# Loading the last output weights of a decode kernel in 32 transfers of 8 partitions instead of 2 transfers of 128

## The chip, the cores and the metric

The kernel runs on one core of a Trainium2 chip. The metric is the device time of one execution in microseconds (us), median over several runs. The time before is 1278.78 us (three runs, 1278.07 to 1279.25).

## The reference

One decode step. Attention of one token over a cache of 65536 positions (8 KV heads, 2 query heads to each, head size 256), and beside it a gated feed-forward layer on the same normalised token; both results are added to the token.

```python
xn = layernorm(x)                                  # x: [1, 1, 448]
q = xn @ wq                                        # 16 heads of 256
p = softmax(q @ k_cache^T / 16)                    # k_cache, v_cache: [8, 65536, 256], bf16
o = p @ v_cache
out = x + o.reshape(1, 1, 4096) @ wo + ffn(xn)     # wo: [4096, 448]
```

K and V are 537 MB together, so the kernel is a stream of transfers from HBM. Of `wo`, the rows of the first 7 KV heads are loaded earlier; this study is about those of the last head, 448 KB, called `wo_end`.

## The kernel before

The parts that matter are at the end of the stream. V of the last head comes in pieces that get smaller, so that little work is left when the last one lands. `wo_end` comes behind them on the same queue (that of SP, the sync engine). The buffer `kt_all` that takes it is free long before.

```python
def item(key, parts, need=()):                     # queues transfers on SP
        for n in need:
            W("sp", *n)
        for ap, src, sem in parts:
            semtot[sem] = semtot.get(sem, 0) + 16
            items[key] = (sem, semtot[sem])
            prog["sp"].append(("d", here[0], ("DMA", key, len(prog["sp"])), (ap, src), sem))
# ...
def wo_src(h):
    return A_wo[h * rep * Dh:(h + 1) * rep * Dh, :].rearrange("(i p f) n -> p i f n", i=rep, f=NH)

def wo_view(t):
    return t.rearrange("p (i f n) -> p i f n", i=rep, f=NH)
# ... the queue's end; LAST = [64, 32, 16, 8, 4, 4], rep = 2, P = 128:
    slot_item("v", NT + 1, 1, None, [("FREE", NU - 1)])
    slot_item("v", NT + 2, 0, None, [("VFREE", NT)])
    slot_item("v", NT + 3, 2, [("last%d" % k if k < len(LAST) - 1 else "slot2", J) for k, J in enumerate(LAST)], [("ATTN",), ("FFN2",)])
    for i in range(rep):
        item(("wo_end", i), [(wo_view(wo_end)[:, i, :, :], wo_src(Hkv - 1)[:, i, :, :], "we%d" % i)],
             [("H", 0), ("H", 1)] if i == 0 else ())
# ... and how an entry of the queue is issued:
                eng.dma_start(fn[0], fn[1]).then_inc(sems[sem], 16)
```

The final product on PE (the TensorE) waits for the first half (semaphore `we0`), multiplies, waits for the second (`we1`) and multiplies again:

```python
        values(NT + 2)
        values(NT + 3)
        dve_ob(T)
        pe_oT(T)
        W("pe", "OTSB", T)
        for i in range(rep):
            W_item("pe", ("wo_end", i))

            def f(it, i=i):
                wo = wo_view(wo_end)
                for hf in range(NH):
                    for g in range(NF):
                        ins = mm(fin(g), lhsT=oT_sb[:, hf, i:i + 1], rhs=wo[:, i, hf, g * DQ:(g + 1) * DQ], start=False,
                                 stop=(i == rep - 1 and hf == NH - 1), tile_position=(0, 32 * g), skip_group_check=True)
                return ins

            O("pe", ("FIN", i), f)
        W("dve", "FIN", rep - 1)
```

Each `wo_end` transfer takes 128 rows of 1792 B, one to each partition. The profile of this kernel shows 256 packets of 1792 B for the two of them and, on each of `we0` and `we1`, 16 increments that came from DMA (1270.82 to 1272.80 and 1271.42 to 1273.36 us). The page counts 16 DMA engines, so this is read as one increment from each engine, after 8 rows. PE waits for 16.

## Time and profile before

| What | Value | Where it is read |
|---|---|---|
| time, median | 1278.78 us | timed runs |
| span of the profiled execution | 1276.0 us | page |
| last V transfer landed | 1272.23 us | semaphore records of the trace |
| `wo_end` landed, first and second half | 1272.80, 1273.36 us | semaphore records |
| from the last V to the last `wo_end` ("the tail") | 1.13 us | difference |

The page of the kernel before. The row DMA is the busy share of the 16 DMA engines in tenths, in 40 slices of the span; the last line is the chain of waits, by engine:

```profile
span 1276.0 us, 23620 instructions
...
DMA  9999999999999999999999999999999999999998
GB/s 405 430 428 440 437 431 436 431 429 440 433 429 438 427 440 433 431 438 427 436 436 431 438 429 431 438 431 431 438 427 438 436 431 438 427 436 438 409 434 360
DMA packets 13588, 549.20 MB, mean 430 GB/s; under 512 B 1414, under 2 KB 3464, under 8 KB 4104
...
DMA 76%; PE 19%; SPq 2%; ACT 1%; issue 1%; DVE 1%; ACTq 0%; DVEq 0%
```

The DMA engines are busy throughout, and the chain of work that ended last is three quarters DMA. So a change at the queue's end matters only through the last few microseconds. These are, in order of time, in the chain of waits of the kernel before (start, length, what; all in us):

```profile
by line: DMA ring<-in_A_v_cache_dram 82.2%; SPq L883 4.4%; PE ps_t L412 2.8%; PE ps_s L412 2.0%; PE ps_m L412 1.1%; issue 0.9%; DVE kt_all L835 0.8%; DVE oT_sb L654 0.4%; SPq L877 0.0%
...
1233.60 38.63 DMA ring<-in_A_v_cache_dram
...
1272.28 0.49 PE ps_m L412 x12
...
1273.02 0.94 PE ps_s L412 x8
...
1273.98 0.38 DVE kt_all L835
```

The last V, 0.5 us of PE, 0.2 us of DVE, then the final product with `wo_end` (`ps_s`). The timeline of the same stretch has the waits in brackets: the engine's idle time before the group, and what ended it.

```profile
1272.28 0.38 PE L412 MATMUL ps_m<-p_sb,ring 128*128 128x2 bf16 x8 [0.25 <-DMA ring<-in_A_v_cache_dram]
...
1272.80 0.16 DVE L654 TENSOR_TENSOR oT_sb<-ps_m,rs 128x4 bf16<-128x4 f32 x1 [0.48 <-PE ps_m L412]
...
1273.02 0.92 PE L412 MATMUL ps_s<-kt_all,oT_sb 128*1 128x224 bf16 x8 [0.25 <-DVE oT_sb L654]
1273.40 0.09 PEld L412 LDWEIGHTS ps_s<-kt_all,oT_sb 128*1 128x1 bf16 x4 [0.30 <-DMA kt_all<-in_A_wo_dram]
1273.98 0.38 DVE L835 CAST kt_all<-ps_s 33x224 bf16<-33x224 f32 x1 [1.02 <-PE ps_s L412]
```

The first half of the product starts as soon as its other operand `oT_sb` is there. The second half's weights waited 0.3 us for `wo_end`. In the list of waits, in us in total, times and longest:

```profile
PEld ps_s L412 <- DMA kt_all<-in_A_wo_dram: 0.3, 1, 0.3
```

And the two transfers by their tile (lengths of issue on SP in ns, minimum, median and maximum; then the time from issue to landing):

```profile
L883 SPq DMA_DIRECT2D kt_all<-in_A_wo_dram x2: 368/400/433, 1234.1 to 1234.5; - x2
...
DMA to landing us min/median/max: 38.7/38.7/38.8
```

So they are issued 38.7 us before they land: they queue behind V. The tail of 1.13 us is their own time on the engines, 16 packets each (75 ns a packet on average, 1.2 us). It is almost hidden behind the 0.7 us of work between V and the final product.

The 16 engines are not in step. From the semaphore records, the times at which each engine reported its share of the last V, and of the second `wo_end` transfer:

```
last V     1270.24 1270.37 1270.49 1270.94 1271.10 1271.52 1271.57 1271.75 1271.80 1271.82 1271.83 1271.87 1271.96 1272.01 1272.22 1272.23
wo_end, 2  1271.42 1271.56 1271.67 1272.08 1272.23 1272.60 1272.66 1272.84 1272.91 1272.93 1272.94 1272.95 1273.07 1273.12 1273.32 1273.36
```

Paired in order of time (the records don't name the engine), each ends 1.1 to 1.2 us after its own V. What counts is the slowest one.

### The profile page before, as it was taken

What the parts mean: (1) busy time and instruction counts of PE and PEld (TensorE: products, weight loads), DVE (VectorE), ACT (ScalarE), POOL (GpSimd) and SP (SyncE); (2) the same over time, 40 slices, a digit from 0 to 9 for tenths busy, and PEclk for the clock granted to TensorE, in tenths of its full rate; (3) what the DMA queues carried; (4) which work ended last, traced back from release to release, by engine and by line L of the source; (5) the groups of instructions that cost most, each with busy time, mean ns of one, the idle gap of its engine ahead of it and who ended that gap; (6) DMA issues with size and microseconds to landing.
All of it is one profiled execution on the core that took longest, in us unless ns stands there. A gap on an engine that the chain in (4) does not pass through costs nothing.

```text
span 1276.0 us, 23620 instructions
## 1 busy us (share of the span) xinstructions
PE 976.1 (76%) x9791; PEld 638.2 (50%) x9791; DVE 570.2 (45%) x1079; ACT 436.6 (34%) x655; POOL 8.0 (1%) x38
## 2 busy tenths in 40 slices
PE   4998888778777679767778776787777688777674
PEld 3676655455544456444555454455454455454321
DVE  4665554355444455343454344454344554444310
ACT  1554533244333334323333342343333334332300
POOL 2000000000000000000000000000000000000000
PEclk9998999799888898887898888898888998888885
DMA  9999999999999999999999999999999999999998
GB/s 405 430 428 440 437 431 436 431 429 440 433 429 438 427 440 433 431 438 427 436 436 431 438 429 431 438 431 431 438 427 438 436 431 438 427 436 438 409 434 360
DMA packets 13588, 549.20 MB, mean 430 GB/s; under 512 B 1414, under 2 KB 3464, under 8 KB 4104
## 3 DMA queue, kind: packets, MB, share of 16 engines
q1 hardware_dynamic: 13570, 549.03, 99.7%
q8 instruction: 8, 0.13, 0.0%
q14 instruction: 4, 0.03, 0.0%
q10 hardware_dynamic: 6, 0.00, 0.0%
HBM read 549.03 MB, written 0.00 MB: 430 GB/s over the span
## 4 chain that ended last, share of the span: by engine, by line
DMA 76%; PE 19%; SPq 2%; ACT 1%; issue 1%; DVE 1%; ACTq 0%; DVEq 0%
DMA ring<-in_A_v_cache_dram 70%; PE ps_o L412 13%; DMA ring<-in_A_k_cache_dram 5%; PE ps_t L412 3%; SPq L883 2%; PE ps_m L412 2%; PE ps_q L412 2%; ACT kt_all L482 1%; DMA ring<-in_A_wo_dram 1%; DVE kt_all L480 0%; ACT S_sb L563 0%; PE ps_s L412 0%; DVE kt_all L699 0%; DVE m1p L533 0%; DVE kt_all L835 0%
## 5 line engine op out<-in xcount | busy, mean ns | idle before, releaser
L412 PE MATMUL ps_t<-ident_f,ring 128*128 128x128 f32 x4096 | 590.0, 286 | 71.9 <-DMA ring<-in_A_k_cache_dram 48.3
L480 DVE COPY kt_all<-ps_t 128x1024 bf16<-128x1024 bf16 x768 | 486.9, 684 | 285.8 <-PE ps_q L412 281.2
L412 PEld LDWEIGHTS ps_t<-ident_f,ring 128*128 128x128 f32 x4096 | 453.9, 144 | 227.6 <-issue 139.8
L482 ACT ACTIVATE kt_all<-ps_t 128x1024 bf16<-128x1024 bf16 x256 | 262.2, 1024 | 507.0 <-PE ps_q L412 506.9
L412 PE MATMUL ps_o<-ring,p_sb 128*4 128x512 bf16 x2044 | 186.9, 531 | 195.6 <-DMA ring<-in_A_v_cache_dram 191.3
L412 PEld LDWEIGHTS ps_o<-ring,p_sb 128*4 128x4 bf16 x2044 | 55.2, 105 | 289.5 <-issue 265.7
L412 PE MATMUL ps_q<-kt_all,q_cur 128*2 128x512 bf16 x2056 | 164.7, 397 | 0.6 <-DVE kt_all L480 0.6
L504 ACT ACTIVATE s<-ps_q 98x512 bf16<-98x512 f32 x257 | 151.8, 591 | 1.3 <-PE ps_q L412 1.3
L588 DVE RECIPROCAL rs<-ps_m 128x4 f32<-128x4 f32 x29 | 5.3, 183 | 271.8 <-PE ps_m L412 271.8
L573 ACT ACTIVATE p_sb<-S_sb 128x128 bf16<-128x128 bf16 x64 | 18.9, 307 | 266.2 <-PE ps_o L412 266.0
L412 PEld LDWEIGHTS ps_s<-sel_bf,s 128*128 128x128 bf16 x1032 | 64.2, 97 | 6.3 <-ACT s L504 1.9
L412 PE MATMUL ps_s<-sel_bf,s 128*128 128x8 bf16 x1032 | 63.4, 167 | 2.3 <-ACT s L504 1.3
L631 DVE CAST ob_sb<-ps_o 100x512 bf16<-100x512 f32 x29 | 20.1, 692 | 100.7 <-PE ps_o L412 100.7
L412 PEld LDWEIGHTS ps_q<-kt_all,q_cur 128*2 128x2 bf16 x2056 | 26.4, 79 | 45.5 <-issue 45.5
L412 PEld LDWEIGHTS ps_m<-rowsum,ones_f 128*128 128x128 f32 x116 | 20.1, 246 | 20.5 <-issue 20.5
L412 PE MATMUL ps_m<-rowsum,ones_f 128*128 128x2 f32 x116 | 22.5, 299 | 0.0
L533 DVE TENSOR_REDUCE m1p<-S_sb (+1 forms) x33 | 13.9, 422 | 4.4
L482 ACT ACT_TABLE_LOAD x7 | 9.0, 1283 | 19.1 <-PE ps_q L412 19.1
L531 DVE CAST S_sb<-ps_s 128x256 f32 (+1 forms) x33 | 13.6, 414 | 1.9 <-PE ps_s L412 1.9
L563 ACT ACTIVATE S_sb<-S_sb,negmax 128x512 bf16<-128x512 bf16 x16 | 13.2, 852 | 3.0 <-DVE negmax L557 3.0
L412 PE MATMUL ps_m<-diag,ones_f 2*128 2x2 f32 x58 | 11.0, 256 | 3.7 <-DVE diag L548 0.6
L412 PEld LDWEIGHTS ps_m<-diag,ones_f 2*128 2x128 f32 x58 | 8.5, 182 | 10.5 <-DVE diag L548 10.5
(94 smaller groups left out, 129.3 us busy)
## 6 DMA issues: line engine op xcount, KB each, us to landing
ring<-in_A_k_cache_dram SPq DMA_DIRECT2D x10, 4096.0 KB, 35.1
ring<-in_A_v_cache_dram SPq DMA_DIRECT2D x1, 4096.0 KB, 30.9
ring<-in_A_wq_dram SPq DMA_DIRECT2D x1, 3584.0 KB, 11.3
ring<-in_A_wo_dram SPq DMA_DIRECT2D x7, 448.0 KB, 17.1
ring<-in_A_v_cache_dram SPq DMA_DIRECT2D x1, 2048.0 KB, 35.5
ring<-in_B_w_gate_dram SPq DMA_DIRECT2D x1, 1568.0 KB, 14.9
ring<-in_B_w_up_dram SPq DMA_DIRECT2D x1, 1568.0 KB, 18.3
ring<-in_B_w_down_dram SPq DMA_DIRECT2D x2, 784.0 KB, 20.5
```

What stands on the lines that cost most here:

```text
L412: return pe.matmul(*a, **k)
L480: O(e, ("EV", s, m), lambda it: nc.vector.tensor_copy(out=kt[:, :], in_=tb[:, :]), f"ev{m}")
L482: O(e, ("EV", s, m), lambda it: nc.scalar.activation(out=kt[:, :], in_=tb[:, :], func=ACTF.Copy), f"ev{m}")
L504: O("act", ("EVQ", s), lambda it: nc.scalar.activation(out=s2[s % 2][0:QROWS, :], in_=ps_q[0:QROWS, :], func=ACTF.Copy), "evq")
L531: O("dve", ("SCOPY", u), lambda it: nc.vector.tensor_copy(out=S_sb[:, at(it, SBN), :], in_=ps_sn), "sc")
L533: O("dve", ("SMAX", u), lambda it: nc.vector.tensor_reduce(out=m1p[:, :, at(it, 1)], in_=S_sb[:, at(it, SBN), :].rearrange("p n i -> p i n ...
L563: O("act", ("EXP", h, i), lambda it, i=i: nc.scalar.activation(out=S_sb[:, :, i], in_=S_sb[:, :, i], func=ACTF.Exp, bias=negmax[:, i:i + 1 ...
L573: O("act", ("PC", t, c), lambda it: nc.scalar.activation(out=p_sb[:, c, :, :], in_=S_sb[:, n:n + CH, :], func=ACTF.Copy), "pc")
L588: O("dve", ("RS", t), lambda it: nc.vector.reciprocal(out=rs[:, :, :], in_=ps_m[0:P, C_TOT:C_TOT + NH * rep]))
L631: O("dve", ("OB", t), lambda it: nc.vector.tensor_copy(out=ob_sb[0:OROWS, :], in_=ps_o[0:OROWS, :]))
L883: eng.dma_start(fn[0], fn[1]).then_inc(sems[sem], 16)
```

## The change

The transfers are cut into groups of 8 partitions, 4 apart. The intent: each transfer then runs on 8 of the 16 DMA engines, the same 8 for all. When the prediction was made this was the author's assumption, and from it comes the estimate of 32 packets to each of the 8 engines; the result below shows 8 increments with the data of each transfer.

```diff
     for i in range(rep):
-        item(("wo_end", i), [(wo_view(wo_end)[:, i, :, :], wo_src(Hkv - 1)[:, i, :, :], "we%d" % i)],
+        ws = [slice(p0 + r, p0 + 32, 4) for p0 in range(0, P, 32) for r in range(4)]
+        item(("wo_end", i), [(wo_view(wo_end)[w, i, :, :], wo_src(Hkv - 1)[w, i, :, :], "we%d" % i) for w in ws],
              [("H", 0), ("H", 1)] if i == 0 else ())
```

There are now 32 transfers instead of 2. Bytes, order and everything else stay.

## The prediction

> **What bounds the kernel now.** The stream of K, V and weights. The page shows DMA busy over 90% in 39 of 40 slices, 549 MB at 430 GB/s, and the chain of waits is 76% DMA. At the end (chain of waits, timeline): the last V transfer is done at 1272.23 us, then PE ps_m 0.49, DVE 0.17, the final product with these weights 0.94, DVE 0.38, output DMA; the span ends at 1276.0.
>
> **What the changed transfers cost now.** The two wo_end transfers (224 KB each, 128 rows of 1792 B) are issued at 1234.1 and 1234.6 (0.37 and 0.43 us of SP each, DMA issues), behind V on the same rings, and land at about 1272.8 and 1273.4. So they trail the last V by only 1.13 us, and the second half of the final product waits 0.3 us for them (list of waits). The trace's semaphore landings show that the 16 engines are out of step: they finish the last V between 1270.24 and 1272.23, and each finishes its own wo_end 1.13 to 1.18 us later: 16 packets of 1792 B at about 0.073 us.
>
> **What the change does.** It makes 32 transfers of 8 rows. [...] Nothing is removed. [...]
>
> Sum for the slowest of the 8 engines (estimate from the trace):
> - 32 x 0.073 = 2.34 us of data, against 1.17: +1.17.
> - 30 more semaphore packets at about 0.010 us: +0.3. At the existing boundaries they do not stall what follows (2048 B packets: 8 in 0.69 us with the semaphore, 0.68 without).
> - [...]
> - [...]
>
> So wo_end's last landing goes from 1273.4 to about 1274.8 (1274.3 to 1275.4), all of it on the critical path, as the final product waits for it. Its first half hides under the wait. SP issues 32 transfers at about 0.4 us, 13 us, from 1234 to about 1248 (or later, if the queue fills up), 22 us before they're needed: off the path.
>
> **Predicted: +2.1 us, 1280.9 us; 8 in 10: 1279.3 to 1286.** Faster by over 2%: 0.005. Within 2%: 0.98. Slower by over 2%: 0.015.
>
> **What would show it.** Last V done within 0.5 us of where it was; wo_end x32, about 0.4 us each, mostly issued by 1250; the wait of the final product (PE ps_s) for wo_end 1.5 to 2 us instead of 0.3, ending about 2.5 us after V; the rest of the profile unchanged.
>
> **What would make it wrong.**
> - SP blocks on a full queue. The issues of the earlier wo transfers blocked for 7.2 and 6.1 us with some 90 descriptors per engine outstanding; here 135 would be. If the last issues come only as V drains, the end is paced by 0.4 us per issue: +5 to +9 us.
> - Semaphore writes packed this densely (one per 0.08 us, each landing 0.47 us after its packet) might serialise: 32 x 0.4, some +10 us.
> - [...]

## The result

The changed kernel takes 1283.47 us (four runs, 1283.27 to 1283.94) against 1279.01 us for the kernel before in the same rounds: 4.46 us more. The ratio is 1.0035, 95% interval 1.0018 to 1.0053. Ratios here and below are the mean time of one kernel's fast runs over that of the other's of the same rounds, so not quite the ratio of the medians.

The page after:

```profile
span 1281.7 us, 23650 instructions
...
DMA  9999999999999999999999999999999999999997
GB/s 406 426 435 440 426 440 429 434 432 440 429 434 432 440 429 434 429 442 429 434 429 442 427 436 429 440 429 434 432 440 427 436 432 440 427 436 432 415 438 281
DMA packets 13812, 549.20 MB, mean 428 GB/s; under 512 B 1638, under 2 KB 3688, under 8 KB 4328
...
DMA 72%; PE 20%; SPq 5%; ACT 1%; issue 1%; DVE 1%; ACTq 0%; DVEq 0%
```

There are 224 packets more, all of 4 B by their records (1413 of them before, 1637 after). That is 32 x 8 - 2 x 16: one semaphore write for each of 8 engines in each of 32 transfers, instead of 16 engines in 2. So the transfers do run on 8 engines each. That they are the same 8 each time is read from the tails below (32 x 0.20 us); which 8 they are, no trace shows. The semaphore records agree with the count: `we0` and `we1` have 144 increments each. Of those of `we1`, 16 come one per transfer, 0.44 us after the end of its issue on SP (the first at 1265.98 us, its issue ended at 1265.54), and the other 128, 8 per transfer, come from 1273.35 us on. PE waits for 256, so by difference each of the 16 early ones must count 8 (an estimate; the records don't hold the amounts).

The timeline after, to be read against the one before:

```profile
1273.76 0.37 PE L414 MATMUL ps_m<-p_sb,ring 128*128 128x2 bf16 x8 [0.22 <-DMA ring<-in_A_v_cache_dram]
...
1274.28 0.16 DVE L656 TENSOR_TENSOR oT_sb<-ps_m,rs 128x4 bf16<-128x4 f32 x1 [0.44 <-PE ps_m L414]
...
1276.21 0.54 PE L414 MATMUL ps_s<-kt_all,oT_sb 128*1 128x224 bf16 x4 [1.96 <-DMA kt_all<-in_A_wo_dram]
1279.09 0.09 PEld L414 LDWEIGHTS ps_s<-kt_all,oT_sb 128*1 128x1 bf16 x4 [2.79 <-DMA kt_all<-in_A_wo_dram]
1279.09 0.54 PE L414 MATMUL ps_s<-kt_all,oT_sb 128*1 128x224 bf16 x4 [2.35 <-DMA kt_all<-in_A_wo_dram]
1279.67 0.38 DVE L837 CAST kt_all<-ps_s 33x224 bf16<-33x224 f32 x1 [5.23 <-PE ps_s L414]
```

The product's operand `oT_sb` is ready at 1274.44. Then its first half waits until 1276.2 and its second half until 1279.1, both for `wo_end`. The list of waits after has both:

```profile
PE ps_s L414 <- DMA kt_all<-in_A_wo_dram: 4.3, 2, 2.3
...
PEld ps_s L414 <- DMA kt_all<-in_A_wo_dram: 2.8, 1, 2.8
```

The last V landed at 1273.72 in this profile (1272.23 before) and the last `wo_end` at 1279.05 (1273.36): the tail grew from 1.13 to 5.33 us. Of the 1.49 us by which V is later, 0.80 were already there at the V transfer that landed 20 us earlier (1253.35 against 1252.55), when no changed transfer had moved a byte. That part is the slowest engine's luck in this run. A second profile of the changed kernel (below) had V at 1272.58 and a tail of 6.39 us, and the same span of 1281.7 us.

The profiled runs lie 5.8 us apart (1283.64 and 1277.88 us), the medians 4.46: the kernel before happened to be profiled in a run 1.1 us below its median. Its times scatter more (1277.9 to 1280.9 us in all rounds) than those of the changed one (1283.3 to 1283.9).

There is a trap in this profile. The chain of waits after ends like this:

```profile
1274.24 0.62 SPq L885
...
1274.91 4.14 DMA kt_all<-in_A_wo_dram
...
1279.09 0.56 PE ps_s L414 x4
...
1279.67 0.38 DVE kt_all L837
```

It runs through SP's issues, 0.62 us each, up to 1274.91, and then gives only the last 4.1 us to the transfer. By tile, the issues took:

```profile
L885 SPq DMA_DIRECT2D kt_all<-in_A_wo_dram x32: 623/624/4798, 1235.0 to 1274.9; - x32
...
  DMA kt_all<-in_A_wo_dram: 7.1, 3
```

Some took up to 4.8 us, which is read here as a full queue (the trace doesn't show how full it was), and the last ended at 1275.53, after V's last landing. The second line is the idle time (us, times) of PE and of its weight loads (PEld) until `wo_end` landed: the 4.3 and the 2.8 us above. One would conclude that SP's issuing paces the end. The experiments below say no.

### The profile page after: what moved, and what is told of

It reads as the page before. It is cut to its first block, busy times and chain, and to the rows that moved or that the text cites. A ratio compares the mean times of both kernels' runs of the same rounds, so it can differ in the third digit from the quotient of the medians.

```text
span 1281.7 us, 23650 instructions
## 1 busy us (share of the span) xinstructions
PE 986.0 (77%) x9791; PEld 641.2 (50%) x9791; DVE 570.4 (45%) x1079; ACT 436.1 (34%) x655; POOL 8.0 (1%) x38
## 4 chain that ended last, share of the span: by engine, by line
DMA 72%; PE 20%; SPq 5%; ACT 1%; issue 1%; DVE 1%; ACTq 0%; DVEq 0%
DMA ring<-in_A_v_cache_dram 66%; PE ps_o L414 13%; DMA ring<-in_A_k_cache_dram 5%; SPq L885 5%; PE ps_t L414 3%; PE ps_m L414 2%; PE ps_q L414 2%; ACT kt_all L484 1%; DMA ring<-in_A_wo_dram 1%; DMA kt_all<-in_A_wo_dram 0%; DVE kt_all L482 0%; ACT S_sb L565 0%; DVE kt_all L701 0%; PE ps_s L414 0%; DVE m1p L535 0%
## 5 line engine op out<-in xcount | busy, mean ns | idle before, releaser
L414 PE MATMUL ps_o<-ring,p_sb 128*4 128x512 bf16 x2044 | 195.5, 550 | 196.8 <-DMA ring<-in_A_v_cache_dram 192.5
```

Of the source, the lines that this page charges most:

```text
L414: return pe.matmul(*a, **k)
```

## The experiments

Three theories of where the tail of 5 to 6 us comes from:

- **T1, a floor per transfer:** an engine needs at least some 0.2 us for each transfer, however few bytes it has. The semaphore records suggest it: at the end of the changed kernel's profile the increments come 0.19 us apart, although a packet of 1792 B takes 0.074 us when nothing holds it up (74 ns at least and 75 on average in the kernel before).
- **T2, bytes:** 8 engines with double bytes each are the limit.
- **T3, the issues:** SP needs 0.62 us per transfer and is held up, for up to 4.8 us in one issue.

All runs gave correct results. "Tail" is always the last landing of `wo_end` after the last of V, from the semaphore records of the run's profile.

### The changed kernel again

No edit; it shared the chip and the runs of the kernel before with the next three.

> The changed kernel unaltered, on the chip of the others of this call. Expected +4.5 us over the kernel before (ratio 1.0035), wo_end landing about 4.5 to 5.3 us after the last V.

Measured: 1283.54 us against 1279.56, ratio 1.0032 (1.0018 to 1.0045). The tail is 6.39 us, which is 32 x 0.200. The last increments of `we1` were at 1277.99, 1278.18, 1278.38, 1278.58, 1278.78 and 1278.97: 0.20 us apart.

The packet records of this profile show the data being held up as well. Of the 256 packets of `wo_end`, 124 took 72 to 100 ns, but 126 took over 150 ns, 187 ns on average; the slow ones begin 1.0 us after the first packet. The last completion came 2.2 us after the last data packet (0.47 us in the kernel before). Read together: the completions first lag behind the data, and when the lag has grown to some 2 us (about 11 transfers at 0.20 us, an estimate from these numbers), the data goes at the same pace. Where the lag stayed below that, at 1.5 us (two packets per transfer, below), no packet was slow.

The timeline:

```profile
1273.14 0.16 DVE L656 TENSOR_TENSOR oT_sb<-ps_m,rs 128x4 bf16<-128x4 f32 x1 [0.46 <-PE ps_m L414]
...
1275.95 0.54 PE L414 MATMUL ps_s<-kt_all,oT_sb 128*1 128x224 bf16 x4 [2.84 <-DMA kt_all<-in_A_wo_dram]
...
1279.02 0.54 PE L414 MATMUL ps_s<-kt_all,oT_sb 128*1 128x224 bf16 x4 [2.54 <-DMA kt_all<-in_A_wo_dram]
```

### Eight neighbouring rows instead of rows 4 apart

```diff
-        ws = [slice(p0 + r, p0 + 32, 4) for p0 in range(0, P, 32) for r in range(4)]
+        ws = [slice(p0, p0 + 8) for p0 in range(0, P, 8)]
```

Only the choice of rows differs from the changed kernel. It tells what the step of 4 partitions is worth.

> Same 32 transfers of 8 rows, but 8 consecutive rows each[...]. If the cost is per transfer on the engine (one data packet, then one semaphore write; 0.19 us apart in the changed kernel), [...] +4.5 us as the changed kernel, within 0.7. [...]

Measured: 1283.89 us against 1279.56, ratio 1.0037 (1.0024 to 1.0051), tail 5.66 us: as the changed kernel. So the step of 4 partitions made no difference to the time that shows. The run also tells on T3. The issues by tile:

```profile
L885 SPq DMA_DIRECT2D kt_all<-in_A_wo_dram x32: 282/322/4796, 1234.8 to 1270.2; - x32
```

A typical issue takes half as long (0.28 us at least and 0.32 in the median, against 0.62; so the step of 4 partitions cost SP 0.3 us each), and the last one ended at 1270.50 us, before V's last landing and some 5 us before the last issue of the changed kernel. The end did not come sooner:

```profile
1279.35 0.53 PE L414 MATMUL ps_s<-kt_all,oT_sb 128*1 128x224 bf16 x4 [2.55 <-DMA kt_all<-in_A_wo_dram]
```

SP's pace is not what counts, although the chain of waits ran through it. T3 falls.

### Sixteen transfers, each with both halves of its rows

```diff
-        item(("wo_end", i), [(wo_view(wo_end)[w, i, :, :], wo_src(Hkv - 1)[w, i, :, :], "we%d" % i) for w in ws],
+        item(("wo_end", i), [(wo_view(wo_end)[w], wo_src(Hkv - 1)[w], "we%d" % i) for w in ws[8 * i:8 * i + 8]],
```

The final product waits for both semaphores before it starts.

> 16 transfers of the same 8 rows 4 apart, each with both halves of a row's weights: the same bytes, engines and packets (2 of 1792 B per engine and transfer), half the semaphore writes and half the issues. Cost per transfer: 16 x 0.19 to 0.26 us, a tail of 3.0 to 4.2 us after V, +2 to +3.5 us over before (0.4 of it because the first half of the product now waits for all). Bytes alone on 8 engines: tail of 2.5 us, +1.7 us. If the pace of SP's issues set the end of the changed kernel, it is gone here, as 16 issues end long before V, and also +1.7 us.

Measured: 1281.30 us against 1279.56, ratio 1.0017 (1.0003 to 1.0031). The tail is 3.30 us, 16 x 0.206. The wait of the final product, now a single one:

```profile
1275.96 0.91 PE L414 MATMUL ps_s<-kt_all,oT_sb 128*1 128x224 bf16 x8 [2.91 <-DMA kt_all<-in_A_wo_dram]
```

The time alone doesn't tell T1 from the bytes (+1.7 was expected of the bytes, +2 or more of T1); the trace does. The last data packet ended at 1274.35 us, its packets took 74 ns on average and none over 80, so no data was held up. The semaphore's last increments came at 1275.43, 1275.63 and 1275.83, 1.5 us later and still 0.20 us apart. In the kernel before, the increment came 0.47 us after the last packet. So with two packets per transfer (0.15 us) the data flows freely and the completions lag, at 0.20 us each.

This run also measures the bytes' part. From V's last landing to the end of the last data packet it is 1.82 us here and 0.66 us before (1272.89 - 1272.23): the doubled bytes on 8 engines cost 1.16 us.

### All 16 engines, small transfers

```diff
+        ws = [slice(p0, p0 + 16) for p0 in range(0, P, 16)]
```

(32 transfers become 16, of 16 rows.)

> 16 transfers of 16 consecutive rows: all 16 engines, the bytes per engine of the kernel before, but 16 semaphore writes per engine instead of 2, each behind one data packet. Cost per transfer: 16 x 0.19 = 3.0 us tail instead of 1.13: +1.5 to +2 us over before. If it is the use of half the engines that costs, and not the small transfers: within 0.3 us of before.

Measured: 1281.03 us against 1279.56, ratio 1.0019 (1.0006 to 1.0033). The tail is 3.16 us, 16 x 0.198, with the last increments at 1275.61, 1275.81 and 1276.00. Each engine has exactly the bytes of the kernel before; only the number of transfers differs. So most of the tail is a matter of small transfers, not of using half the engines, and the floor belongs to an engine: 16 engines incrementing one semaphore keep the same 0.20 us as 8.

### Few transfers on 8 engines: a miss

```diff
+        item(("wo_end", i), [(wo_end.rearrange("p (i x) -> p i x", i=rep)[:, i, :],
+              wo_src(Hkv - 1)[:, i, :, :].rearrange("(e q) f n -> e q (f n)", e=8), "we%d" % i)],
```

> Only 2 transfers as in the kernel before, 128 rows each, but written so that the source's first dimension is 8, which should put them on 8 engines with 16 packets and one semaphore write each (then 8 engine increments per transfer, not 16). If the semaphore writes cost 0.20 us each and the data 0.074 us per packet: tail after V of 32 x 0.074 = 2.4 us plus 0, +1.2 us over before[...]. If half the engines were the cause of the changed kernel's tail: 5 to 6 us, +4.5 us.

Measured: 1278.10 us against 1279.23, ratio 0.9994 (0.9981 to 1.0008), tail 1.12 us. But each transfer's semaphore got 16 increments from engines: the transfers ran on all 16. The split of the source, which is contiguous, had no effect on the number of engines. So this was the kernel before over again, and it serves only to show the scatter: two equal kernels, 1.1 us apart in the medians.

### Transfers of 64 rows

```diff
+        ws = [slice(p0, p0 + 64) for p0 in range(0, P, 64)]
```

> 4 transfers of 64 consecutive rows on 16 engines: 4 packets (0.29 us) to each semaphore write. If a semaphore write lands at most every 0.20 us, it is hidden behind the data: tail 1.1 to 1.3 us, equal to before within 0.4 us. If every transfer adds 0.2 us to its data: tail 4 x 0.49 = 2.0 us, +0.8 us.

Measured: 1280.72 us against 1279.23, ratio 1.0010 (0.9997 to 1.0024), runs from 1279.09 to 1281.60. Inconclusive on the time. The tail is short, 0.88 us, but it starts at a late V (last landing 1273.43), so it proves little. The packet records say more: the last completion came 0.49 us after the last data packet, as in the kernel before (0.47), so no completions queue up where each transfer brings an engine 4 packets (0.29 us). The packets themselves took 103 ns on average and up to 184. Why they took longer, no run shows.

### Twice the transfers, half the bytes in each

```diff
-        item(("wo_end", i), [(wo_view(wo_end)[w, i, :, :], wo_src(Hkv - 1)[w, i, :, :], "we%d" % i) for w in ws],
+        item(("wo_end", i), [(wo_view(wo_end)[w, i, f, :], wo_src(Hkv - 1)[w, i, f, :], "we%d" % i) for w in ws for f in range(NH)],
```

(Neighbouring rows, so that SP issues quickly.)

> 64 transfers of 8 consecutive rows and half a row (896 B): the bytes and the engines of the changed kernel, twice the transfers. At 0.20 us per transfer on each of the 8 engines: tail 64 x 0.20 = 12.8 us, +11 us over before. If the bytes or the 8 engines were the cause: +4.5 us as the changed kernel. If the pace of SP (0.33 us per issue, behind a full queue) decides: 64 x 0.33 = 21 us, of which most before V's end; the end would follow the last issue by under 1 us.

Measured: 1290.04 us against 1279.23, ratio 1.0084 (1.0070 to 1.0098): 10.8 us more. The tail is 12.75 us, 64 x 0.199, from the same bytes on the same engines. The two halves of the product now wait 6 us each:

```profile
1279.27 0.54 PE L414 MATMUL ps_s<-kt_all,oT_sb 128*1 128x224 bf16 x4 [6.03 <-DMA kt_all<-in_A_wo_dram]
...
1285.51 0.54 PE L414 MATMUL ps_s<-kt_all,oT_sb 128*1 128x224 bf16 x4 [5.71 <-DMA kt_all<-in_A_wo_dram]
```

T2 falls as the main cause. SP's last issue ended at 1281.25, 4.2 us before the last landing at 1285.47, so here too it was not the pace.

### The transfers ahead of the last V instead of behind it

The 32 transfers (neighbouring rows) are moved in front of the last V pieces in SP's queue.

```diff
+    for i in range(rep):
+        ws = [slice(p0, p0 + 8) for p0 in range(0, P, 8)]
+        item(("wo_end", i), ...)
     slot_item("v", NT + 3, 2, [("last%d" % k ...
```

> The 32 transfers of 8 consecutive rows are issued before the last V transfers instead of after them (both wait for the same things or less). If the semaphore writes hold up their engine, V on the slowest engine ends up to 6.4 us later than before, and the whole is +4 to +6 us. If only the semaphore writes lag while data goes on, they are hidden under V's 20 us: V ends 2.4 us later than before (its engines' bytes), the wait for wo_end is gone, and the whole is +1.5 to +2.5 us.

Measured: 1284.26 us against 1279.23, ratio 1.0040 (1.0026 to 1.0053). The chain of waits no longer has a wait for `wo_end`, but V ends at 1278.60:

```profile
1251.65 26.95 DMA ring<-in_A_v_cache_dram
...
1278.65 0.50 PE ps_m L413 x12
...
1279.38 0.93 PE ps_s L413 x8
```

That is 6.4 us later than in the profile before. The engines' last reports of V are 6.8 us apart (1271.81 to 1278.60; 2.0 before). The packet records show where the time went. The 256 packets of `wo_end` took 143 ns each, 4.6 us for each of 8 engines instead of 2.4; and eight 32 KB packets of V took 1.9 to 2.3 us, against 1.22 in the kernel before. V's other packets of that stretch were slower too, up to 1.6 us; no run explains this. So data behind a run of 32 small transfers is held up with them: the floor is time of the engine, and moving the transfers forward doesn't hide it.

### Two semaphores in turn

```diff
-        item(("wo_end", i), [(..., "we%d" % i) for w in ws],
+        item(("wo_end", i), [(..., "we%d" % (k % 2)) for k, w in enumerate(ws)],
```

> As the 32 transfers of 8 consecutive rows, but alternate transfers count on two semaphores (the product waits for both before it starts). If 0.20 us is what one engine needs for any semaphore write that follows data: spacing 0.20 us per engine over both semaphores, tail 6 to 6.4 us, +4.5 to +5 us over before. If it is increments of the same semaphore that queue up: tail about 3.2 us, +1.5 to +2 us.

Measured: 1284.32 us against 1279.22, ratio 1.0042 (1.0025 to 1.0058), tail 6.38 us. The last increments, of the two semaphores:

```
we0  1277.88  1278.28  1278.68  1279.08
we1  1278.08  1278.48  1278.88  1279.27
```

Each comes every 0.40 us, both together every 0.20 us. So the floor is not a queue at one semaphore.

### Half of the transfers from another queue

The second half's 16 transfers are issued by ACT on its own queue, after its last work.

```diff
+        item(("wo_end", i), [] if i else [...])
# ... at the end of ACT's program:
+        for k in range(16):
+            w = slice(8 * k, 8 * k + 8)
+            prog["act"].append(("d", ..., (wo_view(wo_end)[w, 1, :, :], wo_src(Hkv - 1)[w, 1, :, :]), "we1"))
```

> The second half's 16 transfers are issued by ACT, on its own queue, after ACT's last work at about 1260 us, while V still streams from SP's queue; the first half's 16 stay behind V on SP's. If the 0.20 us belongs to the engine whatever the queue: the time is lost to V as in the run that put the transfers ahead of V, V ends about 3 us later, then a tail of 3.2 us: +4 to +5 us. If it belongs to the queue: ACT's transfers hide beside V, which loses only their bytes (1.2 us), and the tail is that of 16 transfers, 3.2 us: +2.5 to +3.5 us.

Measured: 1283.51 us against 1279.22, ratio 1.0034 (1.0018 to 1.0051): +4.3 us. ACT's transfers landed between 1262.9 and 1274.2, beside V. V ended at 1275.20, 2.6 us later than in the second profile of the changed kernel (1272.58), and the 16 transfers of SP then had a tail of 3.24 us:

```profile
1275.76 0.16 DVE L657 TENSOR_TENSOR oT_sb<-ps_m,rs 128x4 bf16<-128x4 f32 x1 [0.70 <-PE ps_m L415]
...
1278.57 0.91 PE L415 MATMUL ps_s<-kt_all,oT_sb 128*1 128x224 bf16 x8 [2.85 <-DMA kt_all<-in_A_wo_dram]
```

2.6 us lost before V's end and 3.2 after it: the sum of 5.9 us is nearly that of 32 transfers in one queue (6.4). The time alone, with its interval, would also fit the other answer. V's own packets decide: those of 2 to 16 KB at the end took 178.5 us in sum, against 162 to 169 in the other profiles, so completions of ACT's queue held up data of SP's. The floor holds over the queues of an engine.

### All bytes on one engine

```diff
+        ws = [slice(0, 61), slice(61, P)]
```

> 4 transfers of 61 and 67 rows[...]: all 256 packets on one engine and only 4 semaphore writes. The bytes' term by itself: 256 x 0.074 = 18.9 us tail if that engine ends V last, down to 17 if it ends V first; +15.5 to +17.8 us over before. Should the rows be spread over more engines, the tail is shorter in proportion.

Measured: 1293.18 us against 1279.22, ratio 1.0109 (1.0092 to 1.0126): 14.0 us more, a little under the range. Each transfer had exactly one increment from an engine, so the 61 rows and the 67 rows each went to one engine. The 256 packets ran from 1270.31 to 1288.52, which is 0.071 us per packet (their records average 0.075 and overlap a little), and the last completion came 0.45 us later. Measured from the last V it is a tail of 16.08 us. In these transfers of 61 and 67 packets the engine's time was that of its bytes, and nothing beside them shows.

### Left open

What in a transfer takes the 0.20 us, its semaphore write or something else that each transfer has once, could not be separated: a variant whose extra transfers carry no semaphore does not compile. Eight engines with few transfers could not be had either (the miss above), so the bytes' part on 8 engines rests on the packets of the run with 16 transfers.

The tails together:

| Run | transfers per engine | data per transfer and engine | tail, us | tail per transfer, us |
|---|---|---|---|---|
| before | 2 | 8 packets, 0.59 us | 1.13 | 0.57 |
| changed, two profiles | 32 | 1 packet, 0.074 us unhindered (0.13 on average in these runs) | 5.33, 6.39 | 0.17, 0.20 |
| neighbouring rows | 32 | 1 packet | 5.66 | 0.18 |
| two semaphores | 32 | 1 packet | 6.38 | 0.20 |
| both halves in one | 16 | 2 packets | 3.30 | 0.21 |
| 16 rows, 16 engines | 16 | 1 packet | 3.16 | 0.20 |
| half rows | 64 | half a packet | 12.75 | 0.20 |

The tail starts at the slowest engine's V. Where that engine isn't one of the 8, or not the one that ends last, the quotient comes out below 0.20. This could explain the 0.17 and 0.18: in these two profiles the last engine reported V 1.4 and 1.0 us after the third last one (0.15 us in the second profile of the changed kernel). The last increments were 0.19 and 0.20 us apart in them too.

## Why the prediction was right, and where it was not

The time lay in the range (1279.3 to 1286) and was more than twice the 2.1 us forecast. It lay there because the range was kept wide for the listed ways to be wrong; the sum itself got the bytes right and missed the largest term, so that it lay there is partly luck. Point by point:

- **8 engines, 32 transfers, off-path work unchanged:** right (224 packets more; DMA as busy as before until the last slice).
- **Bytes, +1.17 us:** right. 1.16 us in the packets of the run with 16 transfers.
- **"30 more semaphore packets at about 0.010 us: +0.3. At the existing boundaries they do not stall what follows":** this is the step that failed. The semaphore packets' records are still 9 ns long, but a long run of transfers goes no faster than one per 0.20 us on each engine, and it does stall what follows: the data packets took 0.13 us on average, and the last completion came 2.1 to 2.2 us after the last of them (0.47 before). The tail of 6.39 us, less the old 1.13 and the 1.17 for bytes, leaves 4.1 us for this term instead of 0.3. The boundary that the estimate was read from had 8 packets (0.68 us) to a semaphore write, and so could not show a floor of 0.20. The case was among those listed as making the prediction wrong ("might serialise"), with 0.4 us per write and 10 us; the measured floor is half of that, and part of it overlaps the data.
- **`wo_end` landing at 1274.3 to 1275.4:** outside. It landed at 1279.05 and 1278.97 in the two profiles. The half microsecond to either side of 1274.8 was the author's estimate. The step of 4 partitions that the change brought in has no part that shows: neighbouring rows took the same time within 0.4 us.
- **SP issues at 0.4 us, done by about 1248, off the path:** wrong in the numbers (0.62 us where nothing held it up, 4.8 at most, and the last ended at 1275.5), right in the conclusion: with the last issue 5 us earlier the kernel was no faster.
- **The final product's wait of 1.5 to 2 us, 2.5 us after V:** the right place and the wrong size: 4.3 us in its two halves, and 5.3 us from V to the last landing.

There was little to gain: before, a packet took 75 ns on average and the `wo_end` transfers trailed V by 1.13 us, of which the final product waited 0.3. The gain was at most that 0.3 us. No experiment pointed to a version faster than the kernel before.

## What to carry to other kernels

Count transfers per DMA engine, not only bytes: here an engine needed the larger of its bytes' time and 0.20 us per transfer, so a transfer should bring each engine at least that much data (by these numbers, an estimate, three packets of 1792 B) wherever the queue is on the critical path. Putting small transfers earlier in the queue, on another queue or on other semaphores does not hide this, as the data behind them is held up too (by 32 transfers, or 16 from the other queue, in these runs). And a chain of waits that runs through an engine's issues doesn't prove that the issues are the pace: make them cheaper and look again.
